# Summing keys and values with the key features stationary, and placing the blocks with DMAs

## The chip, the core and the metric

The kernel runs on one core of one Trainium2 chip. Time is device time in microseconds (us) of one execution, lower is better. The kernel before was run twice without the profiler, and one more execution was recorded by the hardware profiler.

## What is computed

Both halves take the same layer-normalised input xn (2048 tokens, 448 features), and their results are added to it. The change is in the first half, a linear attention with 16 heads of 28:

```
q, k, v = split(xn @ wqkv)                         # 16 heads of 28
pq, pk  = q @ w_phi[h], k @ w_phi[h]               # per head, 28 x 28
phi_q   = concat(softmax(pq), softmax(-pq))        # 56 features per head
phi_k   = concat(softmax(pk), softmax(-pk))
kv      = sum over tokens of phi_k^T v             # 56 x 28 per head
z       = sum over tokens of phi_k                 # 56 per head
o       = (phi_q @ kv) / (phi_q . z + 1e-6)
A       = o @ wo
```

The second half is an MLP: gelu(LN(xn) @ w1), token shifts by 1 and 2, @ w2, a residual, then gelu(LN(x1) @ w3) @ w4 with a residual. The output is xn + A + B.

## The kernel before

All five engines follow one list of operations that a small recorder (class Recorder) holds. Each helper (mm and tr for TensorE, act for ScalarE, ew for VectorE and GpSimd, dma for a transfer) appends an operation to its engine's stream in program order, with what it reads and writes. From overlaps of 32-byte pieces of a row in the SBUF tensors, and of whole PSUM banks, the recorder works out which semaphores each operation waits for. No scheduler reorders anything: each engine works its own stream in the order written, and an operation that waits holds up everything behind it on its engine. Every DMA has a semaphore of its own. In the profile all matmuls have line L186, transposes L190, ScalarE L194, VectorE and GpSimd L198 and DMAs L201, so groups are told apart by tile names. Tiles that share storage are shown under the region's name (w for the w1 region, hi for the upper half of the query features, vaug for the scratch of the numerators, phik for the MLP's hidden activations).

The tokens are worked in 16 tiles of 128 or in four groups of 512. The stages:

- Loads, layer norm, transposes of xn (xn_T), the folding of w_phi into the projections (fold), w1 (w1_chunk) and the first eight value tiles.
- The key stage, a loop over i = 0 to 17. It issues k_tile(i), then kv_tile(i - 2), then a value tile (v_tile, i even) or w2_tile (i odd), then q_chunk. From i = 12 on it also issues g_T, which transposes input of the MLP's second half. k_tile projects 128 tokens to 448 key columns, takes exp(x) and exp(-x) on ScalarE into phik, sums each softmax of 28 and takes reciprocals on VectorE, and scales phik in place on GpSimd. kv_tile then adds this tile's contribution to the sums: per group c of four heads, 128 value columns of vaug (each head 28 values, a column of ones that gives z, and three unused) are the stationary operand, and 224 columns of phik move. Four accumulators of 224 columns lie in banks 6 and 7.
- The join. kv_copy moves the two banks to SBUF (kvT, in the region of w1) with two VectorE copies. kv_blocks transposes the eight 112-column pieces on TensorE, so that the features lie on partitions, and one VectorE multiply with a mask writes the diagonal blocks of four heads into kvq.
- The last stage, a loop over g = 0 to 3 of w3_chunk(g, fc), with other work put between its 14 chunks from a list (fill). For g = 0 the list begins with g_apply for four tiles (GpSimd), kv_blocks, num_tile(0), w2_tile(8), g_T(4), num_tile(1), and so on. num_tile(i) multiplies the query features of a tile with all eight blocks of kvq (s = 0 for exp(x), s = 1 for exp(-x), four groups c each) into banks 5 and 6, and VectorE and GpSimd normalise; o_T transposes the result, and fin_tile, four tiles later, multiplies with w4 and wo and writes the output with one DMA.

The storage of phik has a row of 896 per token tile: 448 columns for exp(x), then 448 for exp(-x). kvq is cleared once near the start by GpSimd, which also writes ones into column 29 of each block's own rows for the softmax sums of the queries.

Of the kernel before, what the change touches and what calls it, by code (L numbers as in the profile page):

```python
# [5 lines left out]
ACT = mybir.ActivationFunctionType  # L6
ALU = mybir.AluOpType
# [196 lines left out]
def bass_parallel_sum__linear_kernel_hedgehog__mixer_s_mlp__prompt_kernel(  # L204
    nc, A_x, A_wqkv, A_w_phi, A_wo, B_x, B_w1, B_w2, B_w3, B_w4, out,
):
    _, S, D = A_x.shape
    H, DH = A_w_phi.shape[0], A_w_phi.shape[1]
    F = B_w3.shape[1]
    assert (S, D, H, DH, F) == (2048, 448, 16, 28, 1792)  # L210
    NT, NG, KC, NC, NM, FC, HP = 16, 4, 4, 4, 4, 14, 32
    CR = 112
# [5 lines left out]
    with es:  # L218
        R = Recorder(nc, es)
        total = [0]  # L220

        def region(name, nbytes):
            nbytes = -(-nbytes // 64) * 64
            total[0] += nbytes
            h = es.enter_context(nc.sbuf_tensor(name, [128, nbytes // 2], BF16))
            R.track(h, nbytes)
            return h

        def view(h, cols, dt=BF16, at=0):
            a = h[:, at // 2:at // 2 + cols * DTB[dt] // 2]  # L230
            return a if dt == BF16 else a.bitcast(dt)

        def new(name, cols, dt=BF16):
            return view(region(name, cols * DTB[dt]), cols, dt)

        banks = []
        for b in range(8):
            t = es.enter_context(nc.psum_tensor("bank%d" % b, [128, 512], F32))
# [8 lines left out]
        hT_r = region("hT", NM * HW * 2)  # L247
        hT = view(hT_r, NM * HW).rearrange("p (m s) -> p m s", m=NM)
        phik_r = region("phik", NT * 2 * D * 2)
        phik = view(phik_r, NT * 2 * D).rearrange("p (t s c) -> p t s c", t=NT, s=2)  # L250
        vaug_r = region("vaug", NT * 512 * 2)
        vaug = view(vaug_r, NT * 512).rearrange("p (t c) -> p t c", t=NT)
        gT = new("gT", 2 * KC * 512).rearrange("p (b c s) -> p b c s", b=2, c=KC)
# [10 lines left out]
        w1_r = region("w1", KC * D * 2)  # L264
# [4 lines left out]
        w4 = new("w4", FC * D).rearrange("p (c d) -> p c d", c=FC)  # L269
        g_tok = new("g_tok", 4 * 512).rearrange("p (b d) -> p b d", b=4)  # L270
        kvq = new("kvq", 8 * 128).rearrange("p (b e) -> p b e", b=8)
        kvT = view(w1_r, NC * 224).rearrange("p (c f) -> p c f", c=NC)
        ident = new("ident", 128)
        maskb = new("maskb", CR)
        rsel = new("rsel", CR)
# [40 lines left out]
        def tview(b, n=512, base=0):  # L316
            return b[:, :].bitcast(BF16)[:, base:base + n]

        dve, pool = "DVE", "POOL"
# [35 lines left out]
        mb = maskb[0:CR, :].rearrange("p (h e) -> p h e", h=4)  # L355
# [16 lines left out]
        kq = kvq[0:CR, :, :].rearrange("p b (h e) -> p b h e", e=HP)  # L372
# [65 lines left out]
        def rot_b():  # L438
            return bank(*rot[0])
# [8 lines left out]
        def k_tile(i):  # L448
            b = rot_b()
            for kc in range(KC):  # L450
                R.mm(b[:, 0:D], xnT[:, kc, 128 * i:128 * i + 128], wpk[:, kc, :], kc == 0, kc == KC - 1)
            R.act(phik[:, i, 0, :], b[:, 0:D], ACT.Exp)
            R.act(phik[:, i, 1, :], b[:, 0:D], ACT.Exp, scale=-1.0)
            ph = phik[:, i, :, :].rearrange("p s (h e) -> p (s h) e", e=DH)
            r = i % 4
            R.ew(dve, "tensor_reduce", ksum[:, r, :], ph, axis=AX.X, op=ALU.add)
            R.ew(dve, "reciprocal", rks[:, r, :], ksum[:, r, :])
            R.ew(pool, "tensor_tensor", ph, ph, rks[:, r, :].unsqueeze(2).to_broadcast([128, 2 * H, DH]), op=ALU.mult)

        def kv_tile(i):  # L460
            for c in range(NC):
                R.mm(banks[6 + c // 2][:, 224 * (c % 2):224 * (c % 2) + 224].rearrange("p (s f) -> p s f", s=2),
                     vaug[:, i, 128 * c:128 * c + 128], phik[:, i, :, CR * c:CR * c + CR],
                     i == 0 and c % 2 == 0, i == NT - 1)

        def kv_copy():
            for h in range(2):
                R.ew(dve, "tensor_copy", kvT[:, 2 * h:2 * h + 2, :],
                     banks[6 + h][:, 0:448].rearrange("p (c f) -> p c f", c=2))

        def kv_blocks():
            b = banks[6]
            tv = tview(b, 1024).rearrange("p (b e) -> p b e", b=8)
            for c in range(NC):
                for s in range(2):
                    R.tr(tv[0:CR, 2 * c + s, :], kvT[:, c, CR * s:CR * s + CR], ident[:, :])
            R.ew(dve, "tensor_tensor", kq[:, :, :, 0:DH + 1],
                 tv[0:CR, :, :].rearrange("p b (h e) -> p b h e", e=HP)[:, :, :, 0:DH + 1],
                 mb[:, :, 0:1].unsqueeze(1).to_broadcast([CR, 8, 4, DH + 1]), op=ALU.mult)

        def q_chunk(g, c):
            b = rot_b()
# [101 lines left out]
        for i in range(NT + 2):  # L584
            if i < NT:
                k_tile(i)
            if i >= 2:
                kv_tile(i - 2)
            if i < NT:
                if i % 2 == 0:  # L590
                    v_tile(8 + i // 2)
                else:
                    w2_tile(i // 2)
                    if i % 8 == 7:
                        ln_scale(mv2, rs2, i // 2 - 3, 4)
                q_chunk(*divmod(i, 4))
                if i == 9:
                    for j in range(4):
                        g_apply(j)
                if i >= 12:  # L600
                    g_T(i - 12, banks[5])
                    rot[0] = (0, 1, 2, 3, 4)
        kv_copy()
        R.ew(pool, "memset", o_tok[:, :, D:512], 0.0)
        rot[0] = (3, 4)
        for g in range(NG):
            fill = []
            if g + 1 < NG:
                fill.append(lambda g=g: [g_apply(4 * g + 4 + j) for j in range(4)])
            if g == 0:  # L610
                fill.append(kv_blocks)
            for j in range(4):
                i = 4 * g + j
                fill.append(lambda i=i: num_tile(i))
                if g >= 1:
                    fill.append(lambda i=i - 4: fin_tile(i))
                if g < 2:
                    fill.append(lambda i=i + 8: w2_tile(i))
                    if j == 3:
                        fill.append(lambda i=4 * g + 8: ln_scale(mv2, rs2, i, 4))  # L620
                if g + 1 < NG:
                    fill.append(lambda i=i + 4: g_T(i, banks[7]))
                if i > 0:
                    fill.append(lambda i=i - 1: o_T(i))
            n = 0
            for fc in range(FC):
                w3_chunk(g, fc)
                while n < len(fill) * (fc + 1) // FC:
                    fill[n]()
                    n += 1  # L630
# [33 lines left out]
```

The softmax here doesn't subtract the row's maximum and nothing guards it: scores larger than these inputs give would overflow.

## Time and profile before

| what | value |
|---|---|
| runs without profiler | 233.85 and 234.75 us, median 234.3 |
| profiled execution, first to last instruction (span) | 231.3 us |
| the profiled execution's own time | not listed beside its span; the runs are 3.0 us above the span |
| mean granted TensorE clock | 0.984 |
| share of the chain that ended last | PE 62%, DVE 20%, POOL 7%, ACT 5%, DMA 3% |
| key stage | about 48 to 95.3 us |
| join | 94.9 to 99.5 us |

Busy shares are over the whole span. Matmuls overlap, so the distance from one start to the next tells what a matmul costs in a stream; its own duration is longer. PEld is the loading of the stationary operand, which overlaps the matmuls. In the timeline a row merges neighbouring operations of one kind: start, duration, engine, line, operation, output<-inputs, shapes, count, and in brackets how long the engine stood idle before it and what released it. SPq and ACTq are the instruction queues that issue DMAs.

### The profile page before, as it was taken

The page shows a single profiled execution, that of the slowest core. Times are in us where ns is not written, and L with a number is a line of the kernel's source. Part 1 is how long each engine was busy: PE and PEld are TensorE (multiplying, and loading weights), DVE is VectorE, ACT ScalarE, POOL GpSimd, SP SyncE. Part 2 cuts the span into 40 slices and gives each one's busy share as a digit, 9 for nine tenths or more (in the row PEclk, how much of TensorE's full clock was granted, in tenths as well). Part 3 has the DMA queues.
Part 4 walks back from the last instruction along what each step waited for, and adds up shares of the span by engine and source line. Part 5 has one row for each costly group of instructions (what it writes and reads, how often), then busy time and mean ns, then how long its engine had stood idle before and what let it go on. Part 6 is the DMA issues. An engine that isn't in the chain of part 4 may idle for free.

```text
span 231.3 us, 3260 instructions
## 1 busy us (share of the span) xinstructions
PE 204.6 (88%) x1289; PEld 115.9 (50%) x1289; DVE 128.1 (55%) x291; ACT 94.8 (41%) x168; POOL 93.1 (40%) x125
## 2 busy tenths in 40 slices
PE   0568989798999999696999889989999999999995
PEld 0545555455666566453545445545555455555452
DVE  6389503048888878686765745743643545244211
ACT  2398493695777756641342312323331233322000
POOL 7816600017558965831157033148113312335220
PEclk9988999999999999998899999999999999999999
DMA  6999800000000000000000000000000000000011
GB/s 175 321 262 288 249 5 0 4 0 0 0 3 0 0 0 3 0 0 0 3 0 0 24 20 0 20 23 0 20 23 20 0 20 23 20 16 4 23 40 40
DMA packets 9580, 9.51 MB, mean 41 GB/s; under 512 B 990, under 2 KB 9118, under 8 KB 9566
## 3 DMA queue, kind: packets, MB, share of 16 engines
q1 hardware_dynamic: 9104, 9.29, 14.1%
q8 instruction: 10, 0.16, 0.3%
q10 hardware_dynamic: 462, 0.03, 0.1%
q14 instruction: 4, 0.03, 0.0%
HBM read 7.48 MB, written 1.84 MB: 40 GB/s over the span
## 4 chain that ended last, share of the span: by engine, by line
PE 62%; DVE 20%; POOL 7%; ACT 5%; DMA 3%; issue 2%; SPq 1%; DVEq 0%
PE bank L186 57%; DVE vaug L198 8%; PE bank L190 5%; DVE st L198 5%; POOL phik L198 3%; DMA hi<-in_A_wqkv_dram 3%; DVE xn L198 2%; DVE mv L198 1%; DVE ksum L198 1%; DVE gT L198 1%; POOL vaug L198 1%; POOL xnT L198 1%; POOL g_tok L198 1%; ACT phik L194 1%; ACT hi L194 1%
## 5 line engine op out<-in xcount | busy, mean ns | idle before, releaser
L194 ACT ACTIVATE phik<-bank 128x512 bf16<-128x512 f32 (+1 forms) x88 | 49.1, 580 | 85.9 <-PE bank L186 85.9
L186 PE MATMUL bank<-gT,w 128*128 128x512 bf16 x224 | 57.8, 386 | 0.0
L198 DVE TENSOR_TENSOR vaug<-bank,vaug 128x464 f32<-128x464 f32 (+2 forms) x64 | 33.3, 520 | 38.2 <-POOL vaug L198 25.3
L186 PE MATMUL bank<-w,phik 128*128 128x448 bf16 x224 | 45.0, 352 | 0.0
L198 POOL TENSOR_TENSOR xnT<-vaug 128x448 bf16<-128x448 f32 x16 | 15.1, 941 | 73.8 <-DVE vaug L198 73.8
L198 POOL TENSOR_TENSOR phik<-phik,rks 128x896 bf16<-128x896 bf16 x16 | 27.1, 1697 | 36.3 <-DVE rks L198 36.1
L186 PEld LDWEIGHTS bank<-w,phik 128*128 128x128 bf16 x224 | 21.8, 98 | 20.7
L186 PEld LDWEIGHTS bank<-gT,w 128*128 128x128 bf16 x224 | 20.8, 99 | 18.3 <-issue 1.1
L198 DVE TENSOR_REDUCE ksum<-phik 128x32 f32<-128x896 bf16 x16 | 17.3, 1082 | 18.4 <-ACT phik L194 18.4
L198 POOL TENSOR_TENSOR vaug<-xn,xtok 128x448 f32<-128x448 bf16 x16 | 16.4, 1031 | 6.5 <-DVE vaug L198 6.5
L194 ACT ACTIVATE hi<-bank 112x512 bf16<-112x512 f32 (+1 forms) x20 | 12.4, 680 | 14.9 <-PE bank L186 8.0
L186 PE MATMUL bank<-xnT,w 128*112 128x512 bf16 x64 | 17.0, 407 | 1.5 <-ACT xnT L194 1.5
L186 PE MATMUL bank<-xnT,wpq 128*112 128x512 bf16 x64 | 16.4, 379 | 0.0
L186 PE MATMUL bank<-w,hT 112*128 112x448 bf16 x64 | 14.8, 353 | 0.0
L186 PE MATMUL bank<-wo,xnT 128*128 128x448 bf16 x64 | 14.7, 352 | 0.0
L186 PE MATMUL bank<-wpk,xnT 128*128 128x448 bf16 x64 | 14.7, 352 | 0.0
L198 DVE CAST vaug<-bank 128x448 bf16<-128x448 f32 x16 | 9.5, 593 | 8.6 <-PE bank L186 7.8
L194 ACT ACTIVATE hT<-bank 112x512 bf16<-112x512 f32 x16 | 9.6, 597 | 11.0 <-PE bank L186 10.8
L186 PE MATMUL bank<-wv,xnT 128*128 128x448 bf16 x64 | 13.7, 352 | 0.0
L198 DVE RECIPROCAL vaug<-bank 128x16 f32<-128x16 f32 x16 | 4.1, 257 | 15.2 <-PE bank L186 15.2
L190 PE MATMUL bank<-ident,xnT 128*128 128x128 bf16 x64 | 6.3, 221 | 6.3 <-DVE gT L198 5.6
L186 PE MATMUL bank<-phik,vaug 128*128 128x224 bf16 x64 | 8.8, 259 | 3.2 <-POOL phik L198 3.2
(69 smaller groups left out, 237.3 us busy)
## 6 DMA issues: line engine op xcount, KB each, us to landing
out_dram<-vaug SPq DMA_DIRECT2D x16, 112.0 KB, 1.7
w<-in_B_w_dram SPq DMA_DIRECT2D x1, 1568.0 KB, 17.4
xtok<-in_A_x_dram SPq DMA_DIRECT2D x3, 448.0 KB, 7.6
w<-in_B_w_dram SPq DMA_DIRECT2D x1, 1344.0 KB, 12.7
hi<-in_A_wqkv_dram SPq DMA_DIRECT2D x1, 672.0 KB, 6.3
xtok<-in_A_x_dram SPq DMA_DIRECT2D x2, 224.0 KB, 2.9
w<-in_B_w_dram SPq DMA_DIRECT2D x1, 392.0 KB, 9.0
w<-in_B_w_dram SPq DMA_DIRECT2D x1, 336.0 KB, 6.8
```

The lines of the kernel that those rows point to most:

```text
L186: self.op("PE", lambda e: e.matmul(out, lhsT, rhs, start=start, stop=stop, skip_group_check=True), [out], [lhsT, rhs])
L190: self.op("PE", lambda e: e.transpose(out, in_, ident), [out], [in_, ident])
L194: self.op("ACT", lambda e: e.activation(out, in_, func, **kw), [out], [in_] + aps)
L198: self.op(eng, lambda e: getattr(e, name)(out, *args, **kw), [out], aps)
```

## The change

phik is stored head by head: for each of the 16 heads 28 columns of exp(x) and then 28 of exp(-x). kv_tile makes 128 columns of phik the stationary operand: two heads (112 columns) and 16 columns beyond them; the last takes 16 columns ahead of its two heads. The 64 columns of vaug that belong to the two heads move. There are eight such matmuls per tile in place of four, all in bank 6, and the result has the features on partitions already. kv_copy is one copy of 512 columns to SBUF (kvs). kv_blocks is 12 DMAs on SP's queue, each from kvs to kvq for a set of heads: 28 partitions, 4, 3 or 1 groups, 29 columns (58 bytes). The transposes and the masking multiply are gone. DMAs rather than an engine move the blocks because a head's features have to change partition.

```diff
-        phik = view(phik_r, NT * 2 * D).rearrange("p (t s c) -> p t s c", t=NT, s=2)
+        phik = view(phik_r, NT * 2 * D).rearrange("p (t h s e) -> p t h s e", t=NT, h=H, s=2)
...
-        kvT = view(w1_r, NC * 224).rearrange("p (c f) -> p c f", c=NC)
+        kvs = view(w1_r, 512).rearrange("p (c k e) -> p c k e", c=8, k=2)
...
-            R.act(phik[:, i, 0, :], b[:, 0:D], ACT.Exp)
-            R.act(phik[:, i, 1, :], b[:, 0:D], ACT.Exp, scale=-1.0)
-            ph = phik[:, i, :, :].rearrange("p s (h e) -> p (s h) e", e=DH)
+            bv = b[:, 0:D].rearrange("p (h e) -> p h e", e=DH)
+            R.act(phik[:, i, :, 0, 0:DH], bv, ACT.Exp)
+            R.act(phik[:, i, :, 1, 0:DH], bv, ACT.Exp, scale=-1.0)
+            ph = phik[:, i, :, :, :].rearrange("p h s e -> p (h s) e")
...
         def kv_tile(i):
-            for c in range(NC):
-                R.mm(banks[6 + c // 2][:, 224 * (c % 2):224 * (c % 2) + 224].rearrange("p (s f) -> p s f", s=2),
-                     vaug[:, i, 128 * c:128 * c + 128], phik[:, i, :, CR * c:CR * c + CR],
-                     i == 0 and c % 2 == 0, i == NT - 1)
+            flat = phik[:, i, :, :, :].rearrange("p h s e -> p (h s e)")
+            for c in range(8):
+                at = CR * c if c < 7 else 2 * D - 128
+                R.mm(banks[6][:, 64 * c:64 * c + 64], flat[:, at:at + 128],
+                     vaug[:, i, 64 * c:64 * c + 64], i == 0 and c == 0, i == NT - 1)
 
         def kv_copy():
-            for h in range(2):
-                R.ew(dve, "tensor_copy", kvT[:, 2 * h:2 * h + 2, :],
-                     banks[6 + h][:, 0:448].rearrange("p (c f) -> p c f", c=2))
+            R.ew(dve, "tensor_copy", kvs, banks[6][:, :].rearrange("p (c k e) -> p c k e", c=8, k=2))
 
         def kv_blocks():
-            b = banks[6]
-            tv = tview(b, 1024).rearrange("p (b e) -> p b e", b=8)
-            for c in range(NC):
+            kd = kvq.rearrange("p (c s) e -> p c s e", s=2)
+            kf = kvs.rearrange("p (c q) k e -> p c q k e", q=2)
+            for k in range(2):
                 for s in range(2):
-                    R.tr(tv[0:CR, 2 * c + s, :], kvT[:, c, CR * s:CR * s + CR], ident[:, :])
-            R.ew(dve, "tensor_tensor", kq[:, :, :, 0:DH + 1],
-                 tv[0:CR, :, :].rearrange("p b (h e) -> p b h e", e=HP)[:, :, :, 0:DH + 1],
-                 mb[:, :, 0:1].unsqueeze(1).to_broadcast([CR, 8, 4, DH + 1]), op=ALU.mult)
+                    p = 2 * DH * k + DH * s
+                    for q, a, n, off in ((0, 0, 4, 0), (1, 0, 3, 0), (1, 3, 1, 16)):
+                        j = 2 * q + k
+                        R.dma(kd[DH * j:DH * j + DH, a:a + n, s, HP * j:HP * j + DH + 1],
+                              kf[p + off:p + off + DH, a:a + n, q, k, 0:DH + 1])
```

## Prediction, made before the changed kernel was run

> **What bounds the kernel now.** I read the page's engine line first: PE is the engine to watch, but 88% is an average over stages.
>
> ```profile
> span 231.3 us, 3260 instructions
> PE 204.6 (88%) x1289; PEld 115.9 (50%) x1289; DVE 128.1 (55%) x291; ACT 94.8 (41%) x168; POOL 93.1 (40%) x125
> ```
>
> So next the timeline of PE alone around the edited stage (start, us, line, operation, count, idle before).
>
> ```profile
> 72.24 0.55 PE L186 MATMUL bank<-phik,vaug 128*128 128x224 bf16 x4
> 72.62 0.92 PE L186 MATMUL bank<-w,hT 112*128 112x448 bf16 x4
> ...
> 75.00 0.55 PE L186 MATMUL bank<-phik,vaug 128*128 128x224 bf16 x4
> ...
> 94.90 0.56 PE L186 MATMUL bank<-phik,vaug 128*128 128x224 bf16 x4 [1.74 <-POOL phik L198]
> 95.29 1.89 PE L186 MATMUL bank<-gT,w 128*128 128x512 bf16 x8
> 97.02 0.61 PE L190 MATMUL bank<-ident,w 128*112 128x128 bf16 x8
> 97.47 1.03 PE L186 MATMUL bank<-gT,w 128*128 128x512 bf16 x4
> 98.85 0.62 PE L186 MATMUL bank<-kvq,eq_lo 112*128 112x128 bf16 x8 [0.36 <-DVE kvq L198]
> 99.31 1.03 PE L186 MATMUL bank<-gT,w 128*128 128x512 bf16 x4
> ...
> 107.44 0.40 PE L190 MATMUL bank<-ident,xnT 128*128 128x128 bf16 x4 [2.09 <-DVE gT L198]
> ```
>
> Start to start counts here, as ends overlap. Four kv matmuls take 72.62 - 72.24 = 0.38 us (96 ns each); an iteration takes 75.00 - 72.24 = 2.76 us without a gap, so this stage is PE's. The eight kvq matmuls, each with its own weights, take 99.31 - 98.85 = 0.46 us, 57 ns each. The join of the stages is the chain POOL, kv, copy, transpose, kvq, num_tile. The chain of waits gives its rows:
>
> ```profile
> 93.15 1.71 POOL phik L198
> 94.85 0.05 issue
> 94.90 2.28 PE bank L186 x12
> 97.18 0.46 PE bank L190 x8
> 97.64 0.02 issue
> 97.67 1.14 DVE kvq L198
> 98.81 0.05 issue
> 98.85 0.63 PE bank L186 x8
> ```
>
> VectorE starts num_tile(0) at 99.51, 4.66 us after the last POOL row ended at 94.85. From there to 107.4 the chain is VectorE's, without a hole: whatever delays num_tile(0) delays everything behind it. For the new DMAs I read the rows of the DMA line (min/median/max ns to issue):
>
> ```profile
> L201 SPq DMA_DIRECT2D out_dram<-vaug x16: 332/332/367, 127.1 to 229.1; - x16
> L201 SPq DMA_DIRECT2D xtok<-in_A_x_dram x5: 424/589/767, 0.8 to 8.2; - x5
> L201 ACTq DMA_DIRECT2D wphi<-in_A_w_phi_dram x1: 687/687/687, 0.8 to 0.8; - x1
> ```
>
> An output DMA has 128 runs, the first x load 256, wphi 448 short ones: the cost grows with the runs. An output lands 1.7 us from issue (median).
>
> [...] a load of 128 columns lasts 98 ns, of 112 columns 130. [...] Here the 2.09 us gap before 107.44 is followed by a mean clock of 0.55 from 107.5 to 110 and 0.71 to 112. [...] No SBUF-to-SBUF transfer stands in this trace.
>
> **The change part by part.**
>
> *kv matmuls.* 4 x 224 columns become 8 x 64 per tile, and weight loads double from 64 to 128 in all. [...] the other end is 57 ns, the rate at which kvq's loads are seen to keep up. So a tile takes 0.23 to 0.46 us against 0.38: over 16 tiles -2.4 to +1.2. I take 40 ns[...]: 0.32 us, 16 x -0.06 = **-1.0**. It counts in full where PE is the bound (iterations to 80 us, and again 81.4 to 92.6) and, through k_tile, moves the last POOL row earlier. In the wait of 0.73 at 81.42 POOL is the bound, but that chain starts from k_tile too.
>
> *Exponentials in runs of 28.* Same 448 elements, same count of 32, output now in runs of 28 with a stride of 56. The nearest row with such runs is VectorE's v copy: 593 ns, against 619 for the contiguous copy (groups by form, both from PSUM, 448 columns). I take nothing. Cover: ScalarE issues two pairs per iteration, 1.08 + 0.98 = 2.06 us, under PE's 2.7. Above about 0.3 us more per exp the cover is gone. TENSOR_REDUCE and POOL's multiply still run over the same contiguous 896: nothing.
>
> *Join, removed and added.* Gone: one copy (2 x 0.62 becomes one of 512 columns, 0.69), eight transposes (0.45), the masking multiply (1.14). Added: 12 DMAs on SP, whose queue is empty from 13.8 to 127.1, so nothing is queued behind them that is due. All 12 wait for the copy; on PE everything queues behind num_tile(0): its last matmul reads block c=3, s=1, which needs DMA 12. PE waits in order, so w3 chunks, w2_tile(8), and with them all of VectorE's work, stand behind it. Nothing hides this: VectorE and POOL have no other work that PE doesn't feed.
>
> From the end of the last POOL row: 0.05 issue + 0.10 first load + 8 x 0.04 + 0.21 to VectorE (as kvq's 0.66 less 0.45) = 0.68; copy 0.69; SP 0.03. The DMAs have 112, 84 and 28 runs: by the output's 0.33 (128 runs), about 0.35, plus the 0.05 between issues in the first loads = 0.40 each. Eleven of them before the twelfth: 4.40. Landing 1.70. Last matmul, its load and the way to VectorE: 0.30. Sum 7.8, against 4.66: **+3.1**. Bounds of a step: 0.31 (fewer runs cost less) to 0.69 (as wphi, also 28 partitions with short runs): -1.0 to +3.2. Landing 1.3 to 2.4: -0.4 to +0.7.
>
> *Clock.* PE runs out at 97 and first restarts when DMA 8 lands, 3 us later, for four matmuls, then waits again. After that it should be at half clock. w3 and w2_tile(8) then take twice their 0.86 + 0.76 (99.31 to 100.17 to 100.93 in the timeline), VectorE (2.3 us of num_tile(0), 99.51 to 101.83) waits about 1.0, perhaps 2.2 if num_tile(1) is late as well. Against that, in the kernel before VectorE idles 2.12 us before 110.42 (all engines' timeline), behind w3 and num_tile(2) at half clock; with PE busy later, the 2.09 gap shrinks to about 1, and at full clock this idle is 0.8. So +1.0 to +2.2 less 1.3, or a second cold spell on top: -0.3 to +2. I take **+0.6**.
>
> Sum: -1.0 + 3.1 + 0.6 = +2.7. The profiled span 231.3 becomes 234.0. The two runs have a median of 234.3, 3.0 outside the span; the same 3.0 gives **237.0 us**, +1.2%. About 2% (4.7 us) is what a measurement of this kernel can tell from no change, so the verdict would be within 2%.
>
> **The rivals.**
> *SP's queue is dearer than it looks, slower.* If each of the 12 issues costs 0.69 + 0.05 like wphi, the twelfth starts 11 x 0.34 = 3.7 later: 240.7. It passes 2% from 0.58 per issue on, all else equal. For: 28 partitions and short runs as in wphi. Against: wphi has four times the runs, and x loads with 512 runs cost about as much.
> *ScalarE becomes the bound, slower.* If runs of 28 double an exp (0.49 to 0.98), an iteration becomes 3.04 against 2.70, 14 x 0.34 = 4.8 more: 241.8. Only the VectorE row speaks against it.
> *The narrow matmuls pay for the DMAs, not slower.* At 29 ns (-2.4), and the clock no worse than before (-0.3): 231.3 - 2.4 + 3.1 - 0.3 gives about 234.7 as a time. It decides at kv tiles of 0.24 us. Being faster by 2% would need the DMA chain to vanish, and it cannot: 12 issues at 0.33 alone are 3.6.
>
> **How the numbers follow.** Forecast (235.6 to 238.9) 0.60; dear queue or slow landing 0.15; ScalarE or two cold spells 0.08; paid for 0.14; faster 0.03. The range reaches to both sides, 234.6 to 240.6. Slower over 2%: 0.15 + 0.08 - the part of the queue case under 239 (0.02) = 0.21; faster 0.03; within 2% 0.76.
>
> **What would show it.** 128x64 matmuls spaced about 40 ns, iterations near 2.70; phik exps of 448 still 550 ns; 12 issues in about 4.8 us after one 512-column copy; PE idle before kvq's first matmul near 3 us with DMA as releaser, and num_tile(0)'s first VectorE row at about 101.6; low clock after it. Wrong if issue steps are over 0.58, if the exps are over 0.8, if the iterations don't shorten, or if PE doesn't wait for kvq.

## The result, and the profile after

The changed kernel takes 241.22 us (median of 2 runs, 240.94 and 241.49) against 234.3: a ratio of 1.0305 (241.22 over 234.3 alone is 1.0295), 95% interval 1.0237 to 1.0374. It is slower by some 3%, and lies above the range of the prediction (234.6 to 240.6). The profiled execution took 240.94 us, with a span of 239.2 us: 7.9 more than before. (In the runs further below, medians are over all runs of a kernel, and ratios leave out those more than 1.5% above its fastest.) First the page's engine line of the changed kernel:

```profile
span 239.2 us, 3375 instructions
PE 204.5 (85%) x1332; PEld 113.8 (48%) x1345; DVE 126.4 (53%) x289; ACT 94.8 (40%) x168; POOL 93.1 (39%) x125
```

PE's busy time hardly changed (204.6 to 204.5), and VectorE has less to do. Eight more microseconds with no more work are a wait. The timeline of PE shows where (lines left out are marked; start, us, line, operation, count, idle before it and its releaser):

```profile
71.66 0.40 PE L186 MATMUL bank<-vaug,phik 128*128 128x64 bf16 x8
71.89 0.92 PE L186 MATMUL bank<-w,hT 112*128 112x448 bf16 x4
...
93.87 0.41 PE L186 MATMUL bank<-vaug,phik 128*128 128x64 bf16 x8 [2.04 <-POOL phik L198]
94.33 4.22 PE L186 MATMUL bank<-gT,w 128*128 128x512 bf16 x11
103.50 0.48 PE L186 MATMUL bank<-kvq,eq_lo 112*128 112x128 bf16 x3 [4.95 <-DMA kvq<-w]
104.14 0.26 PE L186 MATMUL bank<-kvq,eq_lo 112*128 112x128 bf16 x1 [0.16 <-DMA kvq<-w]
105.90 0.48 PE L186 MATMUL bank<-kvq,eq_lo 112*128 112x128 bf16 x3 [1.50 <-DMA kvq<-w]
106.77 0.26 PE L186 MATMUL bank<-kvq,eq_lo 112*128 112x128 bf16 x1 [0.39 <-DMA kvq<-w]
```

Eight kv matmuls of 64 columns take 71.89 - 71.66 = 0.23 us, 29 ns each; the four of 224 took 0.38. The loss is ahead of the first kvq matmuls: 4.95 + 0.16 + 1.50 + 0.39 = 7.0 us of idle, all released by the block DMAs, where the kernel before had 0.36. The chain of waits through that stretch (start, us, what) names the engine that made PE wait:

```profile
92.12 1.71 POOL phik L198
93.82 0.05 issue
93.87 0.42 PE bank L186 x8
94.29 0.02 issue
94.31 0.70 DVE w L198
95.02 0.02 issue
95.03 1.04 SPq L201
96.08 0.05 issue
96.12 0.86 SPq L201
96.99 0.04 issue
97.03 0.80 SPq L201
...
103.86 0.81 SPq L201
104.67 0.04 issue
104.71 1.92 DMA kvq<-w
```

After one copy of 0.70 us the chain is SP's queue, issue after issue, and only at its end a transfer. The rows of the DMA line give the price of an issue, which is the time for which one DMA instruction holds its queue (in the chain above the next issue starts 0.04 to 0.05 us after the one before has ended; ns to issue, min/median/max):

```profile
L201 SPq DMA_DIRECT2D out_dram<-vaug x16: 332/332/379, 135.0 to 237.1; - x16
L201 SPq DMA_DIRECT2D kvq<-w x12: 788/816/1042, 95.0 to 104.7; - x12
```

A block DMA of 28 to 112 short runs costs 0.82 us to issue, two and a half times an output of 128 long ones, and hardly less when it has 28 runs (0.79) instead of 112 (0.83).

To set the runs side by side I split the span into four pieces: to the start of the first GpSimd multiply of phik; from there to the end of the last one (the key stage); from there to VectorE's first row of num_tile(0) (the join); and the rest.

| us | to first multiply | key stage | join | rest | span |
|---|---|---|---|---|---|
| before | 51.14 | 43.71 | 4.66 | 131.79 | 231.3 |
| changed | 51.61 | 42.21 | 13.26 | 132.12 | 239.2 |
| difference | +0.47 | -1.50 | +8.60 | +0.33 | +7.9 |

The first piece is the loads and the layer norm, which the change doesn't touch; it was 50.98 to 54.36 in the traces below, so a difference of 0.47 there says nothing.

### The profile page after: what moved, and what is told of

Read it like the earlier page. It is cut to its first block, busy times and chain, and to the rows that moved or that the text cites. A ratio compares the mean times of both kernels' runs of the same rounds, so it can differ in the third digit from the quotient of the medians.

```text
span 239.2 us, 3375 instructions
## 1 busy us (share of the span) xinstructions
PE 204.5 (85%) x1332; PEld 113.8 (48%) x1345; DVE 126.4 (53%) x289; ACT 94.8 (40%) x168; POOL 93.1 (39%) x125
## 4 chain that ended last, share of the span: by engine, by line
PE 60%; DVE 18%; POOL 7%; SPq 4%; ACT 4%; DMA 4%; issue 2%; DVEq 0%
PE bank L186 55%; DVE vaug L198 7%; PE bank L190 5%; SPq L201 4%; DVE st L198 4%; DMA hi<-in_A_wqkv_dram 3%; POOL phik L198 3%; DVE xn L198 2%; DVE ksum L198 1%; DVE mv L198 1%; POOL vaug L198 1%; POOL xnT L198 1%; POOL g_tok L198 1%; ACT phik L194 1%; DVE gT L198 1%
## 5 line engine op out<-in xcount | busy, mean ns | idle before, releaser
L186 PE MATMUL bank<-gT,w 128*128 128x512 bf16 x211 | 56.9, 396 | 0.7
L186 PE MATMUL bank<-w,hT 112*128 112x448 bf16 x64 | 15.5, 367 | 0.0
L186 PE MATMUL bank<-kvq,eq_lo 112*128 112x128 bf16 x64 | 5.8, 227 | 7.0 <-DMA kvq<-w 7.0
```

The lines of the kernel that those rows point to most:

```text
L186: self.op("PE", lambda e: e.matmul(out, lhsT, rhs, start=start, stop=stop, skip_group_check=True), [out], [lhsT, rhs])
```

## The experiments

All are edits of the changed kernel, unless it says otherwise, and the code shown is cut to the main lines; ratios are to the kernel before on the same chip, with their 95% intervals where there are several runs.

**The price of an issue by itself.** The kernel before, with 20 DMAs on SP's queue in the key stage, where it is empty (the remarks stand here alone, not in the kernel):

```diff
...
+                R.dma(r4(part(28)), x4[56:84, :, 0:29])          # 28 partitions x 4 x 29, SBUF to SBUF
+                R.dma(part(28)[:, 0:29], src[56:84, 0:29])       # 28 x 29
+                R.dma(r4(part(32)), x4[56:88, :, 0:29])          # 32 x 4 x 29
...
+                R.dma(part(32)[:, 0:29], x2d[0:32, 0:29])        # 32 x 29, from DRAM
+                R.dma(full()[:, 0:29], src[:, 0:29])             # 128 x 29
...
```

> The kernel before, with 20 extra DMAs on SP's queue in the key stage, where that queue is empty, into storage that nobody reads: ten shapes, each twice. From SBUF: 28 partitions x 4 x 29; 28 x 29; 32 x 4 x 29; 28 x 116; 32 x 29; 16 x 4 x 29; from DRAM: 28 x 29; 32 x 29; from SBUF: 128 x 29; 128 x 4 x 29. Theory A (an issue has a fixed price for these shapes, whatever the number of runs): 28 x 4 x 29 and 28 x 29 both about 0.82 us, as in the changed kernel; what sets the price is seen in the others: if it is the 28 partitions, the 32- and 16-partition shapes cost about 0.33 to 0.45; if it is the source in SBUF, the two from DRAM cost about 0.33 and all others 0.82. Theory B (the queue is held back by slow transfers of short runs): the first issues cost about 0.35 and later ones more, and 128 x 4 x 29 costs most. The time stays at 234.3 in both, since the queue is idle there.

The time was 233.65 us (one run). The issue rows of single probes, picked by their start (28 x 29; then 32 x 29 from DRAM and 128 x 29):

```profile
L201 SPq DMA_DIRECT2D w<-xnT x1: 851/851/851, 46.9 to 46.9; - x1
...
L201 SPq DMA_DIRECT2D w<-in_A_x_dram x1: 362/362/362, 51.4 to 51.4; - x1
L201 SPq DMA_DIRECT2D w<-xnT x1: 524/524/524, 51.8 to 51.8; - x1
```

| shape | source | ns to issue, first and second round |
|---|---|---|
| 28 x 4 x 29 | SBUF | 1044 (first DMA after a long pause), 930 |
| 28 x 29 | SBUF | 851, 851 |
| 28 x 116, one run each | SBUF | 780, 787 |
| 32 x 4 x 29 | SBUF | 707, 677 |
| 32 x 29 | SBUF | 587, 617 |
| 16 x 4 x 29 | SBUF | 678, 668 |
| 128 x 29 | SBUF | 524, 525 |
| 128 x 4 x 29 | SBUF | 687, 686 |
| 28 x 29 | DRAM | 567, 566 |
| 32 x 29 | DRAM | 362, 358 |

Theory B falls: no issue gets dearer for those ahead of it, and 128 x 4 x 29, with the most runs, is not the dearest. The price is put together from the form: with both ends in SBUF about 0.25 more (32 x 29: 0.60 against 0.36), with 28 partitions instead of 32 about 0.2 more (0.57 against 0.36 from DRAM, 0.85 against 0.60 from SBUF), four runs instead of one 0.08 to 0.16 more. It was neither of the two single causes I had offered, but both. The sum is not exact: 28 runs of 232 bytes took 0.78 where 28 of 58 took 0.85, and 28 x 4 x 29 took 0.93 here but 0.83 in the changed kernel. Why is open.

**Six of the 12 on ScalarE's queue.**

```diff
-                              kf[p + off:p + off + DH, a:a + n, q, k, 0:DH + 1])
+                              kf[p + off:p + off + DH, a:a + n, q, k, 0:DH + 1],
+                              "SP" if k == 0 else "ACT")
```

> The changed kernel with six of the 12 block DMAs (k = 1) issued by ScalarE's queue instead of SP's; nothing else differs. Theory A (the serial issue cost of 0.865 us each is the delay): the last issue starts about 6 x 0.865 = 5.2 us earlier, num_tile(0) starts on VectorE near 102 instead of 107.1, and the time falls by 4 to 5 us to about 236.5. Theory B (transfers are slow): [...] num_tile(0) stays within 1 us of 107, time about 240 to 241. ScalarE's GELUs come at most 5 us later, behind w3 chunks that PE has already done.

238.91 us, ratio 1.021 (1.0152 to 1.0268); the join took 10.64 us, 2.6 less than 13.26, not 5.2 less. The chain of waits says why:

```profile
95.53 3.18 PE bank L186 x7
98.70 0.02 issue
98.73 0.60 ACT phik L194
99.32 0.36 ACTq L201
99.69 0.04 issue
99.72 0.84 ACTq L201
```

ScalarE's DMAs stand behind the GELU of the second w3 chunk, and PE is slow with that chunk. SP's last issue began at 100.6, ScalarE's at 103.2. The queue price holds (0.84); my count of what is ahead in ScalarE's order was missing.

**Eight DMAs instead of 12.** The rows of phik are padded with 32 zero columns, so the last pair of heads needs no shift:

```diff
...
-                at = CR * c if c < 7 else 2 * D - 128
+                at = CR * c
...
-                    for q, a, n, off in ((0, 0, 4, 0), (1, 0, 3, 0), (1, 3, 1, 16)):
+                    for q, a, n, off in ((0, 0, 4, 0), (1, 0, 4, 0)):
```

> The changed kernel with rows of phik padded to 928 columns, so that the last head pair needs no shifted columns and 8 DMAs do the work of 12. Theory A (fixed price per DMA): 4 x 0.865 = 3.5 us less before num_tile(0), time about 237.7. Price by runs (my prediction's view): the same 896 runs in fewer DMAs save only four times the fixed part, under 1.5 us, time above 239.7.

237.82 us, ratio 1.0177 (1.0132 to 1.0222). The join took 10.16 us, 3.1 less than 13.26, for four DMAs fewer with the same bytes and runs: a price per DMA, not per run.

**The wait taken away.** The 12 DMAs write to storage that nobody reads, and num_tile reads the cleared kvq, so this kernel leaves the attention sums out of its output:

```diff
-            kd = kvq.rearrange("p (c s) e -> p c s e", s=2)
+            kd = kvx.rearrange("p (c s) e -> p c s e", s=2)
```

> The changed kernel, but the 12 DMAs write to storage that nobody reads, and num_tile reads the cleared kvq (so the attention sums are left out of the output; all operations stay). It takes the wait away and leaves matmuls, copy and DMAs. If the wait is the whole loss: PE goes straight on to num_tile(0) near 97 (the half clock after its gap of 2 us may cost 1), and the time is about 234.3 - 1.0 (kv matmuls) - 2 (join of 4.66 us gone) = 231 to 232. If other parts of the change cost too (exps, narrow matmuls, the DMAs in the background): above 234.

233.19 us, ratio 0.9937 (0.9912 to 0.9962): faster than before, by less than I expected. The 12 issues ran as before (0.82 each), and in the background no cost of theirs shows: the key stage is 42.23, the rest 131.66. So the wait is the whole loss. But the join is 5.21, not 2 to 3: PE had three w3 chunks to do ahead of num_tile(0) anyway, and did them slowly:

```profile
94.58 0.46 PE L186 MATMUL bank<-vaug,phik 128*128 128x64 bf16 x8 [2.04 <-POOL phik L198]
95.25 4.00 PE L186 MATMUL bank<-gT,w 128*128 128x512 bf16 x11 [0.22 <-issue]
99.09 0.61 PE L186 MATMUL bank<-kvq,eq_lo 112*128 112x128 bf16 x8
```

Three chunks take 99.09 - 95.25 = 3.8 us where four matmuls of 512 take 0.86 at full clock, so 2.6 for three (11 of 12 records are in the trace). The copy and the transposes of the kernel before were hidden behind them in good part; to remove them is worth little.

**The changed kernel again**, beside the next three:

> The changed kernel itself, beside the next three on one chip. Ratio to the kernel before near 1.03, as first measured; the eleven issue steps of 0.865 us on SP again.

241.36 us, ratio 1.030 (1.0244 to 1.0355), join 13.24 us.

**PE kept at work through the wait.**

```diff
+        def keep_warm():
+            for _ in range(32):
+                R.mm(banks[5][:, :], w3[:, 0, 0:128], gT[:, 0, 0, :], True, True)
...
+                if i == 0:
+                    fill.append(keep_warm)
```

> The changed kernel, with 32 more matmuls of 512 columns put ahead of num_tile(0) on PE, into a bank that num_tile(0) then overwrites: work for some 7 to 8 us in place of the idle wait, so PE should not fall to half clock. Theory C (the half clock after the wait costs its own time, 1.0 to 2.2 us in my prediction): num_tile(1) starts on VectorE about 3.9 us after num_tile(0) instead of 5.47, and the time falls by over 1 us. Theory D (the stage behind is VectorE's, and a PE that is ahead only idles later and falls to half clock then, as in the kernel before at 107.4): num_tile(1) comes 1.6 us earlier, but at num_tile(2) at most 0.4 of it is left, and the time stays within 0.5 us of the changed kernel's.

241.48 us, ratio 1.0347 (1.0268 to 1.0425): no gain. In its trace num_tile(1) comes 4.03 us after num_tile(0) (5.36 in the repeat of the changed kernel), num_tile(2) 9.81 (11.14), but num_tile(3) 15.59 (16.06); the rest of the span from num_tile(0) on is 131.55 against 132.06. Theory D's end is right, its place isn't: the 1.3 us lasted until num_tile(2) and shrank after that, to about 0.5. In the profiled run one of the 12 issues took 1.39 us, so its join is 13.67; the timed runs lie between 240.37 and 243.61, and a gain of 0.5 could not be seen in them.

**Matmuls in place of the DMAs.** sel holds shifted pieces of the identity between zeros (kv_blocks, inside its loop over s):

```diff
...
+                R.mm(ob[:, :, 0, :], sel[:, 0, s, 56:168], kf[:, :, 0, :], True, False)
+                R.mm(ob[:, 0:3, 1, :], sel[:, 0, s, 0:112], kf[:, 0:3, 1, :], False, False)
+                R.mm(ob[:, 3, 1, :], sel[:, 1, s, 0:112], kf[:, 3, 1, :], False, True)
+                R.ew(dve, "tensor_tensor", kq.rearrange("p (c s) h e -> p c s h e", s=2)[:, :, s, :, 0:DH + 1],
+                     b[0:CR, :].rearrange("p (c h e) -> p c h e", c=4, e=HP)[:, :, :, 0:DH + 1],
+                     mb[:, :, 0:1].unsqueeze(1).to_broadcast([CR, 4, 4, DH + 1]), op=ALU.mult)
```

> The changed kernel's matmuls and phik layout, without the DMAs: six matmuls with shifted pieces of the identity as stationary operand (zeros elsewhere) move the features to kvq's partitions, and two VectorE multiplies with the mask write kvq. Theory A (the DMAs are the whole loss): the key stage keeps its gain of 1.5 us, the join takes copy 0.69 + matmuls about 0.7 + two multiplies 1.2, about as long as before (4.7 us, or up to 1 more while PE is at half clock after its gap of 2.0 us), so about 1 us faster than the kernel before, 233. If the new layout or the narrow matmuls cost something elsewhere: 234.5 or more.

233.05 us, ratio 0.9959 (0.9939 to 0.9979). The key stage is 42.21 again, 1.5 less than before; the join is 5.81, 1.15 more. With the DMAs gone the narrow matmuls are a small gain, so the DMAs are the loss. The change took DMAs because a head's features have to change partition; here TensorE moves them. The windows of this kernel show what eats the rest (us, busy time per engine, then PEclk, DMA share and GB/s):

```profile
93.30:97.00 3.70, 3.68 (x17) 1.55 (x18) 0.69 (x1) 0.60 (x1) 3.47 (x7) 0.54 0.00 0
97.00:99.00 2.00, 2.00 (x20) 1.39 (x19) 1.19 (x2) 1.09 (x2) 0.99 (x2) 0.99 0.00 0
```

PE works without a gap through these 3.7 us, at a clock of 0.54: the eight w3 matmuls ahead of the select matmuls took 3.4 us.

**Eight DMAs on two queues, ahead of ScalarE's GELUs.** Padding and queues as above, four DMAs on each queue, and the call moved up behind the copy:

```diff
...
         kv_copy()
+        kv_blocks()
```

> The padded form with 8 DMAs, four on SP's queue and four on ScalarE's, written ahead of the first GELU of the last stage, so that ScalarE doesn't stand behind a w3 chunk as it did with two queues before. Theory A: three issue steps stand before the last issue instead of eleven, 8 x 0.86 = 6.9 us less: num_tile(0) about 6.3 us after the last POOL row instead of 13.3, time about 234. Theory B (transfers): no better than the two queues or the eight DMAs alone, 237.5 or more. The first GELU comes about 3 us later; w3 chunks have three banks, so PE may wait up to 2 us there, inside the wait for kvq.

236.86 us, ratio 1.0106 (1.0052 to 1.0161). The join took 6.89 us (6.3 expected): with three issue steps in place of eleven 6.4 us of the loss are gone, and theory B is out. The time expected was 234; the rest behind num_tile(0) was 133.23 here, 1.1 more than in the changed kernel. It has the lag of half clock at num_tile(1) (5.71 us behind num_tile(0), 3.90 before; the four matmuls of 448 columns between them took 1.50 us, 0.76 before) and doesn't win it back: num_tile(3) is at 17.27, against 15.83 before. Of the 2.9 us by which the median missed 234, 1.8 are not in this trace, which is of the fastest run (235.03); the other three took 236.7 to 237.1.

**32 partitions instead of 28.**

```diff
-                        R.dma(kd[DH * j:DH * j + DH, a:a + n, s, HP * j:HP * j + DH + 1],
-                              kf[p + off:p + off + DH, a:a + n, q, k, 0:DH + 1])
+                        R.dma(kd[DH * j:DH * j + 32, a:a + n, s, HP * j:HP * j + DH + 1],
+                              kf[min(p + off, 96):min(p + off, 96) + 32, a:a + n, q, k, 0:DH + 1])
```

> The changed kernel with the 12 DMAs over 32 partitions instead of 28: each writes four rows too many into its own columns of kvq (so four wrong features per head enter the numerators, values only; no instruction is added or left out). Theory A with the price list of the probes (28 x 4 x 29 about 0.85 to 0.93 with little spread, 32 x 4 x 29 0.68 to 0.71): about 0.15 less per issue, the eleven steps take 11 x 0.72 = 7.9 instead of 9.5, num_tile(0) 11.6 us after the last POOL row instead of 13.25, time 1.6 lower, about 239.5. If the count of partitions isn't the cause of that part of the price: 241 as before.

```profile
L201 SPq DMA_DIRECT2D kvq<-w x12: 596/602/715, 97.8 to 105.0; - x12
```

0.60 us for an issue instead of 0.82, and a join of 10.59 instead of 13.26. 240.08 us, ratio 1.022 (1.0155 to 1.0286). The saving per issue was 0.2, larger than the 0.15 expected; the DMAs still go to partitions from 0, 28, 56 and 84 on, so the count of partitions is what matters. The whole time says less than the join: in this trace PE stood at half clock from 44.62 to 48.03, in the first piece, which came out at 54.36, the longest of all.

**Matmuls in place of the DMAs, and the gap filled.**

```diff
                 kv_tile(i - 2)
+            if i == NT:
+                w2_tile(8)
...
-                    fill.append(lambda i=i + 8: w2_tile(i))
+                    if i > 0:
+                        fill.append(lambda i=i + 8: w2_tile(i))
```

> The select-matmul version with w2_tile(8) moved from behind num_tile(0) to between the last two kv tiles, where PE waits 2.04 us for GpSimd. PE's gap shrinks to about 1.3 us; if the half clock there comes from the gap's length (1.74 us before without it, 2.04 with it), w3 runs at full clock after the join, and PE reaches num_tile(0) about 1 us earlier after the last POOL row than in the version without the move (5.81). w2_tile(8)'s 1.4 us on VectorE leave the chain behind num_tile(0), but may delay the kv copy by up to 0.8. Sum: -1 to -2, time about 231.5 to 232.5, faster than the kernel before by 0.7 to 1%. If nothing of it holds: 233, like the version without the move.

231.05 us (230.0 to 231.47, 6 runs), ratio 0.9868 (0.9835 to 0.9902): it beats both kernels, the one before by a little over 1%. PE's timeline:

```profile
92.90 0.92 PE L186 MATMUL bank<-w,hT 112*128 112x448 bf16 x4
95.11 0.41 PE L186 MATMUL bank<-vaug,phik 128*128 128x64 bf16 x8 [1.28 <-POOL phik L198]
95.57 1.67 PE L186 MATMUL bank<-gT,w 128*128 128x512 bf16 x7
97.08 0.63 PE L186 MATMUL bank<-w,sel 128*112 128x256 bf16 x6
```

The gap is 1.28 us, the eight w3 matmuls then take 97.08 - 95.57 = 1.5 us (3.4 in the version without the move), and the join is 4.12 instead of 5.81. The granted clock is 1.00 in windows from 93.5 to 99. The rest is 130.22, 1.6 less: w2_tile(8) has left it, and the 1.37 us gap at 105.96 brought no half clock.

The edit does two things, and how much each is worth isn't shown: it shortens the gap, and it takes w2_tile(8) out of the work behind num_tile(0). All six runs had a mean clock of 0.99 or more. Without the move five of 20 runs had 0.993 and the others less, but those five, at 232.55 to 233.33 us, were no faster than the median of 233.05.

## Why the prediction was wrong, step by step

**The step that failed** is the price of the DMAs in the join: "by the output's 0.33 (128 runs), about 0.35, plus the 0.05 between issues in the first loads = 0.40 each. Eleven of them before the twelfth: 4.40". From the first issue at 95.03 to the twelfth at 104.71 it was 9.68, 0.88 each. I had explained the spread of the issue rows (0.33, 0.42 to 0.77, 0.69) by the number of runs, and carried that to the new DMAs. The probes show that runs are the least part. Two properties that the new DMAs have and the output row hasn't decide: both ends in SBUF, and 28 partitions. My upper bound, 0.69 from wphi, has the 28 partitions but a source in DRAM, so it bounded nothing (and it left out the 0.05 between issues). The sum of the join, term by term:

| term, us | predicted | measured |
|---|---|---|
| last multiply to the copy | 0.68 | 0.49 |
| copy and step to SP | 0.72 | 0.72 |
| eleven issue steps | 4.40 | 9.68 |
| landing of the twelfth | 1.70 | 1.92 |
| to VectorE's num_tile(0) | 0.30 | 0.45 |
| sum | 7.8 | 13.26 |

5.3 of the 5.5 us are the one term. The mechanism was right: the serial queue is on the path, all 12 wait for the copy, everything stands behind num_tile(0). It was also one of my rivals, "SP's queue is dearer than it looks", with nearly the right time (240.7), but at a price (0.69) that was still too low and with too small a chance; its span, 237.7, is 1.5 below the measured one. Its argument against, that x loads with 512 runs cost about as much as wphi, was true and pointed at the wrong variable.

**From the span to the time.** I added 3.0 us, the distance between one execution's span and the median of two other runs. Where time and span of the same execution are listed, they are 2.0 to 2.1 apart for the kernel before and 1.7 for the changed one. So this term put the forecast about 1 us too high, and by luck hid that much of the miss: in spans it is 234.0 against 239.2. The rival's time came so close by the same luck.

**kv matmuls.** Predicted 40 ns and -1.0 us; measured 29 ns and -1.5 in the key stage. So the fast end of the range, 0.23 us a tile, was exact, with a new 128-column load for each matmul (98 ns a load, overlapped with the matmuls). Nothing in the trace of the kernel before showed that end, as it has no matmul of 64 columns; a line through its 57 ns at 128 columns and 96 at 224 gives 31 at 64, an estimate that would have been close. But 15 x 0.15 = 2.25 us did not become 2.25: 0.23 went at tile 8 (PE stood from 74.27 to 74.50 until GpSimd was done), 0.21 at tile 10 (0.73 to 0.94) and 0.30 at the last tile (1.74 to 2.04). "It counts in full" was wrong: a faster PE waits longer for GpSimd's multiply.

**Exponentials in runs of 28.** Predicted nothing; 551 ns against 550. Right.

**Clock.** Predicted +0.6 net; the rest came out at +0.33. The inner working was right in part: num_tile(1) came 1.57 later and num_tile(2) only 0.35. What I had missed is the gap ahead of the last kv tile, which grew from 1.74 to 2.04 us: after it PE is at half clock (a mean of 0.63 from 93.87 to 98.5), in eight of the nine traces with this gap. The last section says what sets the ninth apart. In the changed kernel the DMAs hide this half clock; it costs when they are gone (3.4 us for the eight w3 matmuls with select matmuls in their place, 1.5 at full clock).

**The removed work.** I counted the copy, the transposes and the multiply as a gain inside the join. With the wait gone the join is still 5.21: PE's w3 chunks ahead of num_tile(0) were the cover, and nearly the bound.

## What to carry to other kernels

A DMA's issue is work on a queue: when several must follow one another between a result and its reader, count them times the issue price of the same form (which memories at both ends, how many partitions), and measure that price in an idle queue if the trace has no such row. Bytes and runs say little about it: 0.79 us with 28 runs, 0.83 with 112. Before an on-chip rearrangement goes to DMAs, try selection matmuls: six of them and two multiplies replaced 12 DMAs, and the join fell from 13.26 to 5.81 us. And when an engine gets faster, look at how its gaps grow: here one of PE's grew from 1.74 to 2.04 us, and PE ran at half clock after it (a mean of 0.63 from 93.87 to 98.5).

## What the runs showed of the hardware

- In the probes, the first of them (1.04) aside, issue prices on SP's queue lay between 0.36 (32 x 29, from DRAM) and 0.93 us (28 x 4 x 29, SBUF to SBUF). 28 partitions cost more than 32 or 16: 0.93 against 0.68 and 0.67 for 4 x 29 from SBUF (second round), and 0.82 against 0.60 in the changed kernel. Why they cost some 0.2 us more is not shown, nor why SBUF at both ends costs 0.25.
- The clock reads 1.00 or 0.50, and half clock comes in stretches of 3.41 us or a multiple, on one grid for each trace: in the changed kernel from 94.55 to 97.96 and, three stretches long, from 101.38 to 111.62. From 28 us on, in these 12 traces, half clock went with how long PE stood idle within one such stretch, not with the length of a gap alone. Wherever PE was idle for 2.0 us or more of a stretch at full clock, half clock followed (2.09 in the kernel before; 2.09 and 2.83 in the changed one); wherever it was 1.8 or less (1.50 in the kernel before, 1.78 with the probes), full clock stayed, with one exception (1.60 us in two gaps before 44.62, with 32 partitions). In the loads, before 28 us, it doesn't hold: half clock followed 1.73 us of idle in the trace of the kernel before (12.15 to 15.57), and full clock stayed through a whole idle stretch in that of the changed kernel (2.39 to 5.81). Two pairs of equal gaps show it, cut on the grid (us, busy time per engine, then PEclk, DMA share and GB/s). First the 2.04 us gap ahead of the last kv tile, with select matmuls (all of it in one stretch) and with 32 partitions (1.24 and 0.80 in two):

```profile
90.20:93.61 3.41, 1.37 (x24) 1.01 (x23) 2.85 (x6) 2.37 (x3) 2.34 (x3) 1.00 0.00 0
93.61:97.02 3.41, 3.41 (x14) 1.27 (x10) 0.69 (x1) 0.60 (x1) 3.29 (x6) 0.50 0.00 0
...
92.41:95.83 3.42, 2.18 (x24) 1.34 (x20) 3.00 (x6) 2.54 (x6) 2.49 (x2) 1.00 0.00 0
95.83:99.24 3.41, 2.56 (x18) 1.33 (x20) 1.29 (x4) 1.75 (x3) 3.15 (x7) 1.00 0.01 1
```

Then the 2.09 us gap ahead of o_T(0), in the kernel before (one stretch) and in the same code with the probes (0.31 and 1.78), whose rest was 1.2 us shorter (130.55):

```profile
104.31:107.73 3.42, 1.33 (x13) 0.79 (x12) 2.90 (x8) 0.60 (x1) 0.94 (x1) 1.00 0.00 0
107.73:111.14 3.41, 3.41 (x17) 1.76 (x15) 1.08 (x4) 0.60 (x1) 0.00 (x0) 0.50 0.00 0
...
107.20:110.61 3.41, 1.64 (x17) 1.17 (x18) 2.07 (x6) 0.44 (x2) 0.94 (x1) 1.00 0.00 0
110.61:114.00 3.39, 3.34 (x21) 1.60 (x19) 3.07 (x8) 1.45 (x3) 0.88 (x1) 1.00 0.02 5
```

So in these traces it mattered where a gap of this length fell on the grid, which differs from trace to trace; after the filled gap of 1.28 us the clock stayed at 1.00.
